# A new hand-written order, with weight groups loaded out of turn, in a gated linear attention followed by a gated MLP

## The chip, the core and the metric

The kernel runs on one core of a Trainium2 chip. The core has five engines with a queue of instructions each: TensorE (PE in the profile, with weight loads as PEld), VectorE (DVE), ScalarE (ACT), GpSimd (POOL) and SyncE (SP), which issues most transfers between device memory and on-chip memory. An engine takes its instructions in order. The metric is the device time of one execution in microseconds (us).

## The reference

```python
for t in range(S):                       # S = 768, for B = 4 batches and H = 8 heads, D = 48
    state = alpha[:, :, t, :, None] * state + einsum('bhd,bhe->bhde', k[:, :, t], v[:, :, t])
    y[:, :, t] = einsum('bhd,bhde->bhe', q[:, :, t], state)
x = y.transpose(0, 2, 1, 3).reshape(3072, 384)
g = x @ w_gate                           # 384 x 1536
h = g * (1 / (1 + exp(-g))) * (x @ w_val)
return (h @ w_out).astype(float32)       # 1536 x 384
```

Inputs of the attention are float32; the three weights are float64.

## The kernel before

**Attention.** The work is cut into 16 units of 192 tokens (a batch has four), each with all eight heads. A unit loads alpha, k and q (tasks `La`, `Lk`, `Lq`) and v (`V`, two buffers that alternate). Units 0 to 3 are transposed by TensorE (`Ta`, `Tk`, `Tq`, after a widening copy `pa`, `pk`, `pq`), the later ones by VectorE (`tr`, `tk`, `tq`). Two scans on VectorE (`G`, `f`) form running products of alpha; `mk` and `q` scale k and q by them. TensorE makes chunk scores (`S`), `ma` masks them, `B` or `Bw` carries the state on, and `Y` makes the outputs. Outputs are split into a high part and its residue (`yh`, `yl`) and packed into the layout of the MLP, for units 0 and 1 by TensorE (`R`, `x`), for the others by ten transfers (`xr`).

**MLP.** The 3072 tokens make 8 blocks of 384, and the 1536 hidden features 12 tiles f of 128: 96 steps. In a step PE makes the products `g` and `v` (nine matmuls each, since a product of two split numbers takes three); ACT makes `sl`, the silu of `g`; DVE makes `h`, its product with `v`; ACT rounds `h` to the high part `hh`, DVE or POOL makes the residue `hl`; PE adds the pair into the outputs (`o`, nine matmuls). Blocks 0 and 1 run in two halves (steps 0 to 6 are block 0 with f = 0 to 6, steps 7 to 13 block 1; steps 14 to 23 the rest), with half sums kept in device memory in between (`os`, `pl`); blocks 2 to 7 run through. Rows of outputs are copied from PSUM by `ot` and stored by `os`. In the profile a tile such as `h0_5` is block 0, f = 5.

**Weights.** The 36 weight tiles come in 20 groups: groups 0 to 2 hold one tile, the others two. Group p is loaded by `wl{p}` as pairs of 32-bit words and made a float32 by three passes over the words (`w{p}v0`, `v1`, `v2`; function `single`, L157 or L159, L165 or L169, L175); `w{p}a` rounds it to the high part (L343) and `w{p}p` forms the residue (L347). The raw words of group p lie where the finished group p + 1 will lie, so a group cannot be rounded before the next one's raw words have been used.

**Guards.** The fast path holds only for inputs in some range. All weights are loaded again and checked by ACT (`wr`, `wc`, 36 of each), and so is alpha, for each unit (`Lc`, `ck`: two passes, L456 and L457, summed into a column of `viol`). At the end DVE and PE reduce the sums to a flag (L921 to L932); every engine reads the flag (`values_load`, L1083) and branches on it (L1084) past a slow general path.

**What sets the order.** The string `ORDER` names all 1519 tasks in program order, as engine:task, with PSUM banks behind @ (t is TensorE, v VectorE, s ScalarE, g GpSimd, y SyncE). The program runs through it and issues each task on the engine named; each engine's queue is the part of the list that has its letter. Nothing else reorders the instructions.

Of the kernel before, what the change touches and what calls it, by code (L numbers as in the profile page):

```python
# [51 lines left out]
v:ma0.1 v:w1p s:ad0.2 t:Ta3@56 v:G2 y:Lk2 s:w4v0 t:Y0@01 y:Lq2 s:kc1.2 v:de1 s:kc1.1 y:wl10 v:f2 s:yh0.0 t:Bw1@3
s:yh0.1 y:V2 v:yl0.0 g:vc1 v:yl0.1 s:ad1.0 s:ad1.1 g:z2 v:ma1.0 t:R0.2@0 v:ma1.1 t:R0.1@1 v:w2p s:x0.2 t:Y1@47 s:ad1.2
v:w4v1 v:w4v2 s:w5v0 s:x0.1 v:w5v1 t:R0.0@0 v:w5v2 s:yh1.0 s:pk2 y:wl11 v:yl1.0 s:pq2 v:w3v2 t:Tk2@12 s:w5a t:Tq2@34
v:mk2 g:w4a s:w3a y:Lq3 y:wl12 s:x0.0 v:q2 g:w3p t:K2.2@1 s:yh1.1 t:K2.1@0 y:V3 s:kc2.2 t:K2.0@2 v:yl1.1 t:S2@34
s:kc2.1 v:de2 s:ea3 t:R1.1@0 v:ma2.2 g:pk3 t:R1.0@1 s:kc2.0 v:x1.1 t:R1.2@4 v:G3 s:x1.0 t:Tk3@02 s:x1.2 t:Bw2@1 s:pq3
y:wl13 s:vc2 v:mk3 y:wl14 s:w6v0 v:f3 t:Tq3@02 s:qc2 y:wl15 s:ad2.1 t:K3.1@4 t:g0 y:wl16 s:cq3 v:w6v1 y:wl17 s:kc3.1
t:v0 v:ma2.1 g:z3 g:q3 s:sl0 v:ma2.0 y:wl18 s:ad2.0 s:ad2.2 t:Y2@02 v:h0 s:qc3 v:de3 y:Lk4 s:hh0 v:w4p t:S3@13 s:yh2.0
s:yh2.1 v:w6v2 t:K3.0@4 t:K3.2@7 s:w7v0 t:g1 v:ma3.2 g:hl0 s:kc3.0 v:ma3.0 s:kc3.2 g:w6a v:yl2.0 t:v1 s:vc3 v:yl2.1
y:V4 g:w6p v:ma3.1 s:sl1 t:o0 v:h1 s:hh1 v:w5p t:Bw3@0 v:w7v1 s:w8v0 s:w9v0 v:w7v2 t:g2 v:w9v1 s:w7a s:ad3.0 s:ad3.1  # L60
v:w9v2 y:xr2 t:v2 v:w8v1 s:sl2 v:w8v2 t:Y3@01 v:h2 g:w7p s:w9a v:tk4 t:g3 s:hh2 s:yh3.0 s:yh3.1 g:hl1 v:yl3.0 s:w10v0
t:v3 v:yl3.1 v:w9p s:vc4 y:V5 t:o1 s:sl3 v:w10v1 s:w8a v:w10v2 t:g4 v:hl2 s:w10a v:h3 t:o2 v:w10p s:hh3 y:xr3 s:sl4
v:w8p t:v4 v:w11v0 v:w11v1 s:w12v0 t:g5 s:w13v0 v:h4 g:hl3 s:hh4 v:w13v1 t:v5 s:sl5 v:w13v2 t:g6 v:w11v2 y:La5 v:h5
g:hl4 s:w11a t:o3 v:w11p s:sl6 y:La4 t:o4 v:w12v1 s:hh5 s:w14v0 v:w12v2 t:v6 v:w14v1 s:w12a s:w13a v:w14v2 t:g7 v:h6
g:hl5 s:w14a t:v7 s:hh6 v:w14p s:sl7 g:hl6 t:g8 v:h7 g:w12p v:tr4 t:o5 s:sl8 y:Lq4 v:G4 s:w15v0 t:v8 s:hh7 t:o6 v:f4
t:g9 s:ot6.0 s:ot6.1 v:h8 g:hl7 y:os6.0 y:os6.1 s:hh8 t:v9 v:w15v1 s:sl9 v:hl8 t:g10 v:h9 g:z4 g:mk4 t:v10 s:ot6.2
s:sl10 v:w15v2 y:os6.2 t:o7 v:tq4 g:w15a g:w13p t:g11 v:kr4.2 s:hh9 y:Lk5 v:kr4.1 t:o8 g:hl9 s:w16v0 v:h10 g:q4 s:sl11
v:kr4.0 t:o9 s:hh10 v:kr4.3 g:qc4 t:v11 g:w15p v:tr5 t:g12 v:h11 y:Lq5 v:hl10 s:hh11 t:v12 v:G5 s:sl12 t:g13 v:f5
t:S4@01 t:B4@2 v:ma4.2 g:hl11 v:h12 t:o10 s:ad4.0 v:ma4.1 s:sl13 v:w16v1 t:o11 v:w16v2 s:hh12 v:ad4.1 g:hl12 s:w16a
t:v13 v:ad4.2 v:de5 t:o12 v:h13 v:w16p s:hh13 t:g14 v:hl13 v:w17v0 t:v14 v:z5 s:w18v0 y:wl19 v:w17v1 s:sl14 v:ma4.0  # L70
t:o13 v:h14 v:w18v1 s:hh14 t:Y4@01 v:w18v2 s:ot13.0 s:ot13.1 y:os13.0 v:w17v2 y:os13.1 t:g15 s:yh4.0 y:V6 v:tk5 g:w17a
s:vc5 g:hl14 t:v15 s:w18a v:yl4.0 s:sl15 v:w17p s:yh4.1 t:g16 s:ot13.2 v:w19v0 v:h15 g:mk5 y:os13.2 v:yl4.1 s:hh15
y:pl18.0 t:o14 s:sl16 y:La6 v:w19v1 t:v16 v:kr5.3 g:hl15 g:w18p v:tq5 t:o15 v:h16 y:Lk6 t:g17 g:q5 v:kr5.2 s:hh16
v:kr5.0 t:v17 s:sl17 g:qc5 v:hl16 t:g18 v:w19v2 v:h17 s:w19a v:tr6 s:hh17 t:v18 s:sl18 g:hl17 v:kr5.1 y:Lq6 t:o16
v:w19p v:h18 t:S5@01 y:xr4 v:tk6 s:hh18 t:B5@2 g:hl18 v:ma5.2 t:o17 v:ad5.0 v:ad5.1 t:o18 v:ad5.2 v:ma5.0 t:g19
v:ot18.0 v:ma5.1 y:pl18.1 v:G6 t:v19 y:La7 s:sl19 t:Y5@01 v:f6 y:os18.0 t:g20 s:yh5.0 y:V7 v:h19 g:vc6 s:yh5.1 v:yl5.0
# [106 lines left out]
def main_path(ctx, tc, q, k, v, alpha, w_gate, w_val, w_out, out, flag, spill):  # L183
# [137 lines left out]
    def weight_group(pieces):  # L321

        n = len(groups)
        groups.append(pieces)
# [1 line left out]
        is32 = w_gate.dtype == F32  # L330
# [785 lines left out]
```

## Time and profile before

| | before |
|---|---|
| times of three runs | 575.8, 572.19, 572.61 us, median 572.61 |
| the profiled execution: its span, from first to last instruction | 570.8 us |
| PE busy | 545.7 us, 96% of the span |
| DVE, ACT, POOL busy | 391.7, 280.5, 134.0 us |
| first `g` product | 51.67 us |
| end of the last matmul of the last `o` | 564.2 us |
| bytes moved | 77.66 MB, mean 136 GB/s |

The profile is of one execution. Its page gives the busy time of the engines, the busy tenths in 40 slices of the span (14.3 us each), the chain of work that ended last, and the costliest groups of instructions by line of the kernel. A group's row reads: line, engine, operation, out<-in, shapes, count | busy us, mean ns of one | idle before them, and what ended it. "L725" is line 725. The granted clock of TensorE was 0.99 on the mean of the span.

### The profile page before, as it was taken

To read this page: it belongs to the slowest core of one execution; us is meant where nothing else is said; L and a number is where in the kernel's file an instruction comes from. 1 tells how busy PE (TensorE), PEld (TensorE's weight loads), DVE (VectorE), ACT (ScalarE), POOL (GpSimd) and SP (SyncE) were. 2 spreads that over 40 slices of the span, in tenths; PEclk is the share of its full clock that TensorE was granted. 3 is DMA by queue.
4 is the path that set the end of the run, shared out by engine and by line. 5 is a ranking of instruction groups with operands and counts; after the bars stand their busy time and mean duration, and the time that the engine had idled before them with its cause. 6 is when DMAs were issued, how large, how long until landed. Compare 5 with 4: busy or idle time off the path is not lost.

```text
span 570.8 us, 13758 instructions
## 1 busy us (share of the span) xinstructions
PE 545.7 (96%) x5510; PEld 527.4 (92%) x5510; DVE 391.7 (69%) x601; ACT 280.5 (49%) x621; POOL 134.0 (23%) x152
## 2 busy tenths in 40 slices
PE   4779999999999999999999999999999999999995
...
DVE  6899998989989999889889698951793111210211
...
GB/s 204 309 318 254 277 82 112 115 40 108 131 146 146 135 132 107 124 126 113 93 100 187 172 156 205 191 141 89 218 111 85 116 132 86 97 73 121 41 2 47
DMA packets 95367, 77.66 MB, mean 136 GB/s; under 512 B 32832, under 2 KB 92224, under 8 KB 95296
## 3 DMA queue, kind: packets, MB, share of 16 engines
...
## 4 chain that ended last, share of the span: by engine, by line
PE 76%; DMA 10%; DVE 7%; SPq 3%; issue 2%; ACT 1%; DVEq 0%; ACTq 0%
PE ops L757 24%; PE v L725 23%; PE g L725 22%; DMA raw<-in_moe_w_out_dram 3%; DMA raw<-in_moe_w_gate_dram 2%; PE y L652 2%; PE A L580 2%; PE s L556 2%; DMA raw<-in_moe_w_val_dram 1%; DMA L<-in_k_dram 1%; DMA Le<-in_q_dram 1%; DVE K L531 1%; SPq L436 1%; PE y L635 1%; DVE t L165 1%
## 5 line engine op out<-in xcount | busy, mean ns | idle before, releaser
L725 PE MATMUL v<-xT,w 128*128 128x384 f32 x864 | 166.9, 337 | 3.2 <-DVE h L737 2.4
L725 PE MATMUL g<-xT,w 128*128 128x384 f32 x864 | 167.3, 337 | 0.4 <-ACT h L733 0.4
L757 PE MATMUL ops<-w,hh 128*128 128x384 f32 x576 | 159.8, 338 | 0.0
L725 PEld LDWEIGHTS v<-xT,w 128*128 128x128 f32 x864 | 150.7, 188 | 5.8 <-DVE h L737 3.4
L725 PEld LDWEIGHTS g<-xT,w 128*128 128x128 f32 x864 | 150.7, 188 | 1.4 <-ACT h L733 0.7
L737 DVE TENSOR_TENSOR h<-h,v 128x384 f32<-128x384 f32 x96 | 52.9, 551 | 120.1 <-PE v L725 92.5
L746 POOL TENSOR_TENSOR hl<-h,hh 128x384 fp32r<-128x384 f32 x57 | 65.5, 1150 | 264.7 <-ACT hh L741 263.5
L741 ACT CAST hh<-h 128x384 fp32r<-128x384 f32 x96 | 49.1, 511 | 128.1 <-DVE h L737 70.9
L757 PEld LDWEIGHTS ops<-w,hh 128*128 128x128 f32 x576 | 105.5, 188 | 1.0
L757 PE MATMUL ops<-w,hl 128*128 128x384 f32 x288 | 96.8, 336 | 0.0
L733 ACT ACTIVATE h<-g 128x384 f32<-128x384 f32 x96 | 46.9, 489 | 80.6 <-PE g L725 68.8
L531 DVE STREAM_TRANSPOSE K<-Gs 32x384 f32<-32x384 f32 x96 | 54.7, 570 | 2.3 <-PE A L580 0.4
L757 PEld LDWEIGHTS ops<-w,hl 128*128 128x128 f32 x288 | 54.1, 188 | 0.1
L746 DVE TENSOR_TENSOR hl<-h,hh 128x384 fp32r<-128x384 f32 x39 | 22.9, 589 | 14.8 <-ACT hh L741 14.6
L590 DVE TENSOR_TENSOR X<-s,mask 64x384 f32<-64x384 f32 (+1 forms) x48 | 26.3, 552 | 8.5 <-PE s L556 7.6
L471 DVE TENSOR_TENSOR_SCAN AT<-AT,back 128x771 f32<-128x771 f32 x16 | 30.9, 1933 | 0.6
L462 DVE TENSOR_TENSOR_SCAN Gs<-AT,inj 128x772 f32<-128x772 f32 x16 | 28.7, 1794 | 0.1
L417 PE MATMUL pt<-ident,wide 128*128 128x128 f32 x72 | 14.9, 376 | 11.4 <-POOL mask L243 5.1
L417 PEld LDWEIGHTS pt<-ident,wide 128*128 128x128 f32 x72 | 12.1, 197 | 13.4 <-ACT wide L405 5.1
L319 ACT ACTIVATE wc<-wc,wbias 128x384 f32<-128x384 f32 x36 | 23.4, 650 | 1.2
L318 ACT ACTIVATE wc<-wc,wbias 128x384 f32<-128x384 f32 x36 | 23.3, 648 | 1.2
L839 POOL TENSOR_TENSOR Gs<-trk,Gs 128x768 f32<-128x768 f32 x10 | 17.9, 1785 | 25.3 <-DVE Gs L462 13.8
(118 smaller groups left out, 608.4 us busy)
## 6 DMA issues: line engine op xcount, KB each, us to landing
...
```

Source lines behind the costliest of these rows:

```text
L319: nc.scalar.activation(dev, dev, AF.Relu, bias=wbias[:, 1:2], accum_out=wviol[:, 0, i : i + 1])
L417: nc.tensor.transpose(pt[:, j - js.start, :], Wd.rearrange("p j e c -> p (j e c)")[:, j * P : (j + 1) * P], ident)
L462: nc.vector.tensor_tensor_scan(*(x.rearrange("p g t -> p (g t)")[:, ::-1] for x in (Gs, AT, inj)), 0.0, op0=ALU.mult, op1=ALU.add)
L471: nc.vector.tensor_tensor_scan(Af, Af, back[:, 1 : n + 1], back[:, 0:1], op0=ALU.mult, op1=ALU.add)
L531: nc.vector.transpose(out=bass.AP(k0.tensor, k0.offset, [k0.ap[0], (G * 2 * D, NU), (2 * D, G), (1, 32)]), in_=Kg[j * BO + x : j * BO + x ...
L590: nc.vector.tensor_tensor(out=X[r, z, f * GF : (f + 1) * GF, :].rearrange("r g (c t) -> r g c t", c=NU), in0=sps[f][r].rearrange("r g (c t ...
L725: nc.tensor.matmul(pt, wsp[kind, f][a][:, kt * P : (kt + 1) * P], xT[blk][:, b_, kt, :], start=(n == 0), stop=(n == 3 * KT - 1),)
L733: nc.scalar.activation(h, acc.pop(("g", blk, f)), AF.Silu)
L737: nc.vector.tensor_tensor(out=h, in0=h, in1=acc.pop(("v", blk, f)), op=ALU.mult)
L741: nc.scalar.copy(out=hh, in_=acc["h", blk, f])
L746: eng.tensor_tensor(out=hl, in0=acc.pop(("h", blk, f)), in1=hh.bitcast(F32), op=ALU.subtract)
L757: nc.tensor.matmul(ops[blk][i], h[b_][:, i * P : (i + 1) * P], wsp["o", f][a], start=(first and n == 0), stop=(last and n == 2),)
```

## The change

`ORDER` is replaced by another list of the same 1519 tasks. `weight_group` is handed its group's number, where it counted its calls before, so that the loads can stand in any order: it is now 0, 1, 3, 2, 6, 4, 9, 5, 14, 10, 7, 13, 8, 11, 12, 16, 15, 18, 17, 19. The lines behind move up by three (L347 is L344 now, L737 is L734).

By the list, tasks change engines: the residues of groups 0, 1, 2, 4, 10, 11, 14, 16 and 17 go from DVE to POOL, those of 7 and 12 from POOL to DVE; the first cuts of groups 1, 11, 17 and 19 go from DVE to ACT, that of group 0 from ACT to DVE; POOL makes 63 residues `hl` instead of 57; DVE makes 15 copies `ot` instead of 6 and 9 `mk` instead of 6. The load of v for unit 2 stands behind six weight loads on SP's queue, where it stood behind ten. The weight checks `wc` are spread over earlier steps, and the alpha check `ck15` stands at the end of the list.

```diff
@@ -44,97 +44,96 @@
 ORDER = """
-y:La0 y:wl0 y:Lk1 y:La1 y:Lq0 y:V1 s:pa0 t:Ta0@01 s:w0v0 v:w0v1 s:ea0 v:w0v2 y:Lk0 s:w0a v:G0 s:pa1 y:Lq1 s:pq0 y:La2
...
-v:h89 s:hh89 t:v90 s:sl90 v:hl89 t:o89 v:h90 s:hh90 v:hl90 t:g91 t:v91 s:ck14 t:o90 s:sl91 s:ck15 v:h91 t:g92 s:hh91
...
-s:os95.2
+y:La0 s:pa0 y:wl0 t:Ta0@73 y:La1 s:ea0 y:Lq0 s:pa1 y:Lk0 v:w0v0 v:w0v1 v:w0v2 v:G0 t:Ta1@50 s:pq0 s:w0a y:Lq1 y:Lk1
...
+t:o94 y:os83.1 t:o95 v:ot95.0 s:ck13 s:ot95.2 y:os95.0 v:ot95.1 y:os95.1 s:os95.2 v:z15 s:ck15
 """
@@ -282,7 +281,7 @@
     HSEG = 7
-    wsp, groups, wtiles = {}, [], []
+    wsp = {}
     wlist = [("g", 0), ("v", 0)]
     for f in range(1, NF):
@@ -318,14 +317,12 @@
         nc.scalar.activation(dev, dev, AF.Abs, bias=wbias[:, 0:1])
         nc.scalar.activation(dev, dev, AF.Relu, bias=wbias[:, 1:2], accum_out=wviol[:, 0, i : i + 1])
-    def weight_group(pieces):
-        n = len(groups)
-        groups.append(pieces)
+    def weight_group(n, pieces):
         size = len(pieces) * NB
         is32 = w_gate.dtype == F32
         each = NB if is32 else 2 * NB
@@ -871,7 +868,7 @@
     def named_weights(p):
         def load(eng):
-            wfns[p] = weight_group(wgroups[p])
+            wfns[p] = weight_group(p, wgroups[p])
         todo[f"wl{p}"] = load
         if w_gate.dtype != F32:
```

DVE's queue around the sixth and seventh hidden tile of block 0 (`h0_5`, `h0_6`; t11 is the cut of group 11, w11 its split form). Before:

```order
L175 SCALAR_TENSOR_TENSOR t11_1263<-raw11_641,t11_1263 128x768
L737 TENSOR_TENSOR h0_5_1296<-h0_5_1296,v0_5_1286 128x384
L347 TENSOR_TENSOR w11_1317<-t11_1263,w11_1317 128x768
L165 SCALAR_TENSOR_TENSOR t12_1266<-raw12_672,t12_1266 128x768
L175 SCALAR_TENSOR_TENSOR t12_1266<-raw12_672,t12_1266 128x768
L165 SCALAR_TENSOR_TENSOR t14_1348<-raw14_819,t14_1348 128x768
L175 SCALAR_TENSOR_TENSOR t14_1348<-raw14_819,t14_1348 128x768
L737 TENSOR_TENSOR h0_6_1329<-h0_6_1329,v0_6_1351 128x384
```

The same place now:

```order
L174 SCALAR_TENSOR_TENSOR t11_1235<-raw11_947,t11_1235 128x768
L734 TENSOR_TENSOR h0_5_1267<-h0_5_1267,v0_5_1247 128x384
L164 SCALAR_TENSOR_TENSOR t12_1260<-raw12_1034,t12_1260 128x768
L174 SCALAR_TENSOR_TENSOR t12_1260<-raw12_1034,t12_1260 128x768
L394 STREAM_TRANSPOSE trk4_1298<-L1_72 128x4x6x32
L734 TENSOR_TENSOR h0_6_1322<-h0_6_1322,v0_6_1284 128x384
```

The residue of group 11 has left this queue and the cut of group 14 stands behind `h0_6`; the transpose of unit 4's k has come forward.

POOL's queue ahead of the first `hl` (w2 to w4 are weight groups, `wide` a widened unit, X1 the scaled q, L0 and L1 buffers of loads). Before:

```order
L343 CAST w4_667<-t4_458 128x768
L347 TENSOR_TENSOR w3_669<-t3_390,w3_669 128x768
L405 COPY wide_79<-L1_72 128x12x48
L475 MEMSET AT_86 128x3
L490 TENSOR_TENSOR X1_104<-trq3_858,AT_86 112x768
L388 MEMSET L1_72 128x4x32
L746 TENSOR_TENSOR hl0_0_992<-h0_0_880,hh0_0_937 128x384
```

The same place now:

```order
L340 CAST w3_650<-t3_301 128x768
L344 TENSOR_TENSOR w3_650<-t3_301,w3_650 128x768
L402 COPY wide_79<-L1_72 128x12x48
L344 TENSOR_TENSOR w2_613<-t2_529,w2_613 128x384
L487 TENSOR_TENSOR X1_104<-trq3_739,AT_86 112x768
L344 TENSOR_TENSOR w4_840<-t4_601,w4_840 128x768
L385 MEMSET L0_71 128x4x32
L385 MEMSET L1_72 128x4x32
L743 TENSOR_TENSOR hl0_0_984<-h0_0_838,hh0_0_956 128x384
```

The residues of groups 2 and 4 are new here (those of groups 0 and 1 are further up), the rounding of group 4 has gone to ACT, and two memsets of unit 4's loads stand behind group 4's residue.

ACT's queue at the end of the main path (`ops` are the PSUM banks of the outputs, ac13 and ac15 the alpha checks of units 13 and 15). Before:

```order
L741 CAST hh7_10_6784<-h7_10_6737 128x384
L741 CAST hh7_11_6807<-h7_11_6772 128x384
L769 COPY ot7_0_11_6820<-ops7_0_0_6462 128x384
L769 COPY ot7_1_11_6822<-ops7_1_0_6463 128x384
L769 COPY ot7_2_11_6825<-ops7_2_0_6464 128x384
L774 DMA out_0_dram<-ot7_2_11_6825 128x384
L1083 TENSOR_LOAD flag_60
L1084 COMPARE_AND_BRANCH
```

The same place now:

```order
L738 CAST hh7_11_6790<-h7_11_6753 128x384
L453 ACTIVATE ac13_6786<-ac13_6786,nbias_112 128x576
L454 ACTIVATE ac13_6786,viol_110<-ac13_6786,dbias_114 128x576
L766 COPY ot7_2_11_6819<-ops7_2_0_6445 128x384
L771 DMA out_0_dram<-ot7_2_11_6819 128x384
L453 ACTIVATE ac15_6751<-ac15_6751,nbias_112 128x576
L454 ACTIVATE ac15_6751,viol_110<-ac15_6751,dbias_114 128x576
L1080 TENSOR_LOAD flag_60
L1081 COMPARE_AND_BRANCH
```

Two of the three copies of the last outputs have gone to DVE; the check ac13 stands ahead of the third, and the check ac15 between the last store and the reading of the flag.

More of the change, by code (lines that the diff above doesn't have):

```diff
@@ L52 @@
[L52 to L76, printed above, removed]
@@ new lines @@
+v:w3v2 s:kc1.2 v:z2 y:wl6 s:pa3 t:Bw1@4 s:yh0.0 s:w2v0 g:w1p t:Ta3@56 y:wl4 s:vc1 v:yl0.0 s:ad1.1 s:yh0.1 g:pk2
+t:Y1@23 g:pq2 v:w2v1 y:V2 s:ad1.2 v:w2v2 s:w4v0 s:yh1.0 t:Tk2@41 s:w2a s:yh1.1 v:yl0.1 t:R0.1@0 v:mk2 t:Tq2@74 v:q2
+t:R0.0@1 t:K2.0@7 v:yl1.0 y:Lk3 t:R0.2@4 s:x0.0 s:ea3 v:yl1.1 g:w3a s:kc2.0 y:Lq3 s:x0.2 s:pq3 v:x0.1 y:wl9 t:K2.2@2
+t:R1.2@5 t:R1.0@6 t:R1.1@0 v:de2 t:K2.1@4 s:x1.1 v:w4v1 s:x1.0 g:w3p y:wl5 g:pk3 y:wl14 y:V3 t:Tk3@13 y:wl10 s:x1.2
+g:w2p t:Tq3@70 v:G3 v:ad0.0 t:g0 s:kc2.1 v:w4v2 v:f3 s:kc2.2 s:cq3 s:w6v0 t:v0 s:w5v0 s:vc2 t:S2@70 v:w5v1 y:wl7 s:qc2
@@ new lines @@
+t:o2 s:hh3 v:w10v2 s:yh3.1 g:hl3 t:g5 v:yl3.1 v:h4 s:w11v0 t:o3 v:w9p t:v5 s:w10a g:w10p s:w12v0 v:tr4 s:hh4 v:w11v1
+v:w11v2 s:sl5 v:h5 t:g6 v:w12v1 v:w12v2 s:w14v0 t:v6 g:hl4 s:hh5 v:tk4 t:o4 s:w11a g:w11p y:xr3 s:sl6 t:g7 v:h6 v:G4
+s:hh6 s:kc3.2 s:w12a s:w13v0 t:v7 g:hl5 y:Lq4 s:sl7 v:mk4 y:wl16 t:o5 v:w12p v:h7 t:g8 v:f4 g:hl6 g:z4 s:sl8 t:v8 t:g9
+v:w14v1 s:hh7 v:hl7 y:wl15 v:w14v2 v:h8 s:sl9 t:o6 v:ot6.2 v:tq4 s:ot6.0 y:wl18 t:v9 s:hh8 t:g10 v:h9 v:w13v1 g:hl8
+s:w15v0 t:v10 v:w15v1 y:os6.0 v:q4 g:qc4 s:sl10 v:w15v2 s:ot6.1 t:g11 v:w13v2 y:La5 s:w13a t:o7 s:hh9 v:h10 y:os6.1
@@ new lines @@
+s:yh6.0 s:sl26 s:yh6.1 y:pl23.2 v:tr8 s:qc7 v:ot23.1 v:kr7.1 t:g27 v:h26 t:v27 g:hl25 v:yl6.1 s:sl27 v:ot23.2 t:g28
+t:o24 s:hh26 t:o25 v:kr7.3 v:h27 v:tk8 v:yl6.0 v:hl26 s:hh27 g:hl27 v:G8 t:v28 y:os23.1 s:sl28 v:kr7.0 y:V7 t:g29
+s:sl29 t:S7@02 v:f8 v:de7 v:ma7.0 t:B7@1 y:xr6 v:h28 y:wr0 t:o26 s:hh28 v:ma7.1 t:o27 t:v29 v:ad7.0 v:h29 t:g30
+v:ad7.1 v:ma7.2 g:hl28 s:sl30 t:v30 y:V8 v:mk8 s:hh29 s:vc7 t:Y7@02 t:g31 v:kr8.3 v:kr8.0 t:o28 v:hl29 v:h30 s:sl31
+s:hh30 y:wr10 v:kr8.1 y:Lq8 t:v31 v:kr8.2 v:h31 s:yh7.0 y:La9 v:tq8 t:o29 v:yl7.0 v:hl30 y:V9 y:Lk9 s:yh7.1 g:z8 t:g32
@@ new lines @@
+v:tq10 s:ot35.0 s:wc10 v:kr10.2 t:v38 s:sl38 v:h38 v:ma9.2 t:g39 v:ad9.0 y:os35.1 s:hh37 v:ad9.1 y:La11 v:ma9.0
+s:ot35.2 g:hl37 y:Lk11 s:sl39 t:v39 s:wc0 t:o36 v:f10 s:hh38 t:o37 s:vc9 v:h39 v:kr10.0 g:z10 g:q10 t:g40 y:wr2 s:qc10
+g:hl38 v:tr11 v:ma9.1 t:v40 s:sl40 s:hh39 t:g41 y:V10 g:hl39 v:ad9.2 t:S10@12 y:Lq11 v:h40 v:tk11 v:ma10.2 v:ma10.1
+t:o38 t:v41 v:kr10.1 v:G11 s:sl41 v:ad3.0 t:Y9@02 y:wr4 v:mk11 v:h41 s:hh40 s:yh9.0 t:o39 s:wc2 v:de10 v:hl40 t:g42
+t:o40 s:hh41 s:sl42 v:hl41 t:v42 v:kr10.3 v:yl9.0 s:wc4 v:h42 t:B10@0 s:yh9.1 v:yl9.1 t:g43 t:v43 v:ad10.0 v:ma10.0
@@ new lines @@
+g:hl47 v:ma11.1 t:g49 t:o47 v:h48 y:xr10 s:sl49 v:kr12.1 t:v49 v:ma11.2 s:hh48 v:ma11.0 y:wr8 t:Y11@21 s:ot47.1
+s:ot47.0 t:g50 s:yh11.0 y:os47.1 v:h49 v:kr12.2 t:v50 g:z12 s:hh49 v:hl48 s:yh11.1 v:yl11.0 v:hl49 v:kr12.3 y:Lk13
+s:sl50 v:ot47.2 t:g51 t:o48 v:q12 v:tr13 v:h50 s:sl51 s:wc7 t:g52 s:hh50 y:wr5 v:yl11.1 y:xr11 t:o49 t:v51 g:vc12
+y:Lq13 v:tk13 t:S12@01 v:hl50 s:wc5 v:G13 t:B12@2 y:V13 v:ma12.2 v:mk13 s:sl52 t:o50 s:ad12.0 v:h51 v:ad12.1 v:kr13.2
+t:g53 v:ma12.1 g:qc12 s:hh51 g:hl51 t:v52 s:sl53 v:ad12.2 t:o51 v:h52 v:ma12.0 t:g54 s:hh52 t:v53 t:Y12@12 v:hl52
@@ new lines @@
+v:tq13 v:h53 s:wc8 t:v54 v:kr13.1 s:hh53 g:hl53 v:kr13.0 s:sl54 y:wr12 y:La14 v:h54 t:o52 v:de13 v:f13 t:g55 v:z13
+t:v55 s:hh54 s:sl55 v:h55 t:o53 t:v56 g:hl54 g:q13 v:kr13.3 s:yh12.0 s:yh12.1 t:g56 v:yl12.0 v:tr14 y:wr16 s:wc16
+y:wr20 s:hh55 t:o54 t:S13@01 v:yl12.1 s:sl56 v:h56 t:B13@2 v:G14 s:hh56 t:g57 v:ad13.0 s:wc12 g:hl56 s:sl57 y:Lk14
+t:v57 v:hl55 t:o55 v:ad13.1 v:f14 v:h57 y:os47.2 y:Lq14 v:ma13.2 v:ad13.2 t:g58 y:os47.0 y:wr11 t:v58 g:qc13 s:wc11
+g:vc13 v:ma13.1 v:ma13.0 s:sl58 y:wr22 t:Y13@01 s:hh57 g:hl57 v:h58 s:wc20 t:v59 y:wr17 s:yh13.0 v:yl13.0 s:yh13.1
```

121 lines of the change are left out of this document (58 added, 63 removed).

## The prediction

> **What bounds the kernel now.** I read the page first: its span, and the busy tenths of two engines.
>
> ```profile
> span 570.8 us, 13758 instructions
> ...
> PE   4779999999999999999999999999999999999995
> ...
> DVE  6899998989989999889889698951793111210211
> ```
>
> TensorE (PE) is full from the third slice on, so the time is PE's own work plus what PE waits. Next the busy time in three stretches: until the first product of the MoE part (`g0`, at 51.6 us), from there to the start of `g7`, and from there to the last matmul. The columns are the stretch, its length, then PE, PEld, DVE, ACT and POOL busy.
>
> ```profile
> 0.00:51.60 51.60, 36.75 (x699) 32.20 (x700) 42.68 (x65) 38.09 (x82) 12.60 (x36) 0.93 0.93 272
> 51.60:91.60 40.00, 38.11 (x426) 35.70 (x424) 37.01 (x44) 25.55 (x51) 14.06 (x14) 1.00 0.66 181
> 91.60:564.30 472.70, 470.87 (x4390) 459.50 (x4388) 312.04 (x494) 216.44 (x490) 107.30 (x102) 1.00 0.45 118
> ```
>
> PE idles 14.85 us in the first stretch, 1.89 in the second, 1.83 in the third: after 91.6 us nothing but these 1.8 us can be won. What holds PE before that is told by the chain of waits, from 82 us on (start, length, what):
>
> ```profile
> 82.61 0.55 DVE h L737
> 83.16 0.88 DVE t L165
> ...
> 85.64 0.95 DVE t L175
> ...
> 86.62 0.84 ACT w L343
> ...
> 92.78 0.56 DVE h L737
> ...
> 93.38 1.86 PE v L725 x9
> ```
>
> The chain runs along VectorE (DVE): weight cuts (L165, L175), the residue of a split weight (L347), and `h`, on which the next `v` product waits. In the first two stretches DVE is busy 42.7 + 37.0 = 79.7 of 91.6 us. So the front of the program is as long as what stands ahead of `h` in DVE's queue. Behind it PE runs full, and what is won in the front is won at the end, less what the tail costs.
>
> **The front.** The rows of the order in the section on the change show DVE's queue between `h0_5` and `h0_6` (the sixth and seventh hidden tiles of block 0): the residue of group 11 is gone from it, and the cut of group 14 stands behind. POOL's rows ahead of the first `hl` show where residues went: those of groups 0, 1, 2 and 4 are new there. I count DVE's queue up to `h8`, since up to `v9`, which waits for it, PE has the same tasks in both. The durations are means of the first 100 us (group, count, busy, mean ns):
>
> ```profile
> L175 DVE SCALAR_TENSOR_TENSOR t<-raw,t 128x768 uint32<-128x768 uint32 x12 | 13.5, 1131 | 0.3
> L165 DVE SCALAR_TENSOR_TENSOR t<-raw,t 128x768 uint32<-128x768 uint32 x11 | 12.4, 1124 | 0.5 <-ACT t L157 0.4
> ...
> L746 POOL TENSOR_TENSOR hl<-h,hh 128x384 fp32r<-128x384 f32 x7 | 9.6, 1372 | 22.1 <-ACT hh L741 20.9 <-DMA raw<-in_moe_w_out_dram 1.2
> ...
> L347 DVE TENSOR_TENSOR w<-t,w 128x768 fp32r<-128x768 f32 x7 | 8.3, 1196 | 0.9 <-ACT w L343 0.9
> ...
> L347 POOL TENSOR_TENSOR w<-t,w 128x768 fp32r<-128x768 f32 x4 | 8.1, 2031 | 4.7 <-ACT w L343 4.6
> ...
> L490 POOL TENSOR_TENSOR X<-trq,AT 112x768 f32<-112x768 f32 x1 | 1.7, 1697 | 0.9 <-ACT trq L810 0.9
> ...
> L347 DVE TENSOR_TENSOR w<-t,w 128x384 fp32r<-128x384 f32 x3 | 1.6, 544 | 0.0
> ...
> L839 DVE TENSOR_TENSOR Gs<-trk,Gs 128x768 f32<-128x768 f32 x1 | 1.0, 959 | 0.1
> L490 DVE TENSOR_TENSOR X<-trq,AT 112x768 f32<-112x768 f32 x1 | 1.0, 958 | 0.1
> ...
> L746 DVE TENSOR_TENSOR hl<-h,hh 128x384 fp32r<-128x384 f32 x1 | 0.6, 554 | 0.0
> L159 DVE TENSOR_SCALAR t<-raw 128x768 uint32<-128x768 uint32 x1 | 0.6, 552 | 0.0
> ```
>
> Out of the queue ahead of `h8` go the residues of groups 0 to 2 (3 x 0.54 = 1.6) and of 4, 10, 11 and 14 (4 x 1.20 = 4.8), `q1` (1.0), and the two steps of the cut of group 13 (1.12 + 1.13 = 2.25): 9.65. The first step of group 11's cut goes to ACT too (0.55, L159); together 10.2. Into it come the residues of groups 7 and 12 (2.4), `mk4` (1.0, L839), and one `hl` more (0.55): 3.95. Net DVE has 6.2 us less to do.
>
> At `h8` DVE before had a little to spare:
>
> ```profile
> 95.35 0.56 DVE L737 TENSOR_TENSOR h<-h,v 128x384 f32<-128x384 f32 x1 [0.63 <-PE v L725]
> 96.71 1.68 DVE L397 STREAM_TRANSPOSE AT<-L 128x768 f32<-128x768 f32 x1 [0.80 <-DMA L<-in_alpha_dram]
> ```
>
> It waited 0.63 + 0.80 = 1.4 us between `h6` and `h8`, so against the place that did bind, `h6`, the gain is 6.2 + 1.4 = 7.6 us. PE can take that: it idled 16.7 us up to `g7`.
>
> Against it stands that DVE's operations are slower beside POOL's:
>
> ```profile
> 66.94 2.61 POOL L347 TENSOR_TENSOR w<-t,w 128x768 fp32r<-128x768 f32 x1 [4.60 <-ACT w L343]
> ...
> 67.78 2.59 DVE L165 SCALAR_TENSOR_TENSOR t<-raw,t 128x768 uint32<-128x768 uint32 x1
> ```
>
> That cut takes 0.88 to 0.95 us in the chain's rows; here, beside a residue on POOL, 2.59. The three groups of DVE with two inputs (L175, L165, L347) lie above 0.96 (what `q1` and `mk4` took for the same width) by 12 x 0.17 + 11 x 0.16 + 7 x 0.24 = 5.5 us, while POOL worked 9.6 + 8.1 + 1.7 = 19.4 us with two inputs: 0.28 us lost on DVE for each us of POOL. By `h8` POOL has more: residues of groups 0 to 2 (3 x 1.0, half of the wide one) and 4, 10, 11, 14 (4 x 2.03), `q1` 1.7, less groups 7 and 12 (4.06) and an `hl` (1.4): 7.4 us. At 0.28 DVE loses 2.1; at the worst row, 1.64 lost in the 1.77 us in which both ran (0.93), 6.9; at best nothing. I take the mean of the stretch, 2.1.
>
> So the front gives -7.6 + 2.1 = -5.5 us, with ends of -7.6 and -0.7.
>
> The Trainium skill (GPSIMD Engine Reference, section 1, Specifications) speaks against such a move: GpSimd shares its SBUF interfaces with VectorE and contends with Vector instructions that have two SBUF inputs. The row of 2.59 agrees, the mean of 0.28 only in part. If each us of such work were taken from DVE again, as that rule alone would have it, the front would give about -0.7 and the sum would be +2.1.
>
> Two moves are hidden, I think. The load of unit 2's V, which waits for unit 0's outputs, stood behind ten weight groups on SP's queue and stands behind six now, so groups 9, 5, 14, 10, 7 and 13 start up to 15 us later. Their cover is DVE, which cuts them one by one until 92 us; without it each us late costs one. ACT gets three more first cuts and loses copies that move to DVE in the last third, where DVE has room.
>
> **The middle.** One wait in the long third stretch is DVE's again (total, times, longest):
>
> ```profile
> PE v L725 <- DVE h L737: 1.7, 2, 1.2
> ```
>
> With over 6 us less in DVE's queue the longer goes: -1.2. A new order can add stalls of this size; the bounds are -1.8 (all idle gone) and +2.
>
> **The tail.** The guard on alpha for one unit, `ck15`, is two ACT passes; its sum goes into a flag on which every engine branches at the end. As the rows of ACT's end show, `ck15` (tile ac15) moves from `h` of step 91 to behind the last store, and the flag behind it; `ck13` still fits beside the last products. What each takes, from ACT, DVE, the flag's lines and the chain's end:
>
> ```profile
> 540.82 0.77 ACT L456 ACTIVATE ac<-ac,nbias 128x576 f32<-128x576 f32 x1
> ...
> 542.31 0.19 ACT L457 ACTIVATION_READ_ACCUMULATOR ac<-ac,dbias 128x1 f32 x1
> ...
> 564.79 0.38 ACTq L774 DMA_DIRECT2D out_dram<-ot  x1
> ```
> ```profile
> 542.53 0.16 DVE L921 TENSOR_REDUCE vsa<-viol 128x1 f32<-128x16 f32 x1
> ...
> 543.12 0.16 DVE L927 TENSOR_TENSOR oka<-oka,oks 128x1 f32<-128x1 f32 x1
> ```
> ```profile
> L1083 SPq TENSOR_LOAD <-flag x1: 480/480/480, 547.4 to 547.4; - x1
> ...
> L1083 SPq SEQ_ASSERT  x1: 37/37/37, 548.5 to 548.5; - x1
> ```
> ```profile
> L1084 SPq EVENT_SEMAPHORE  x8: 17/17/17, 568.9 to 569.4; - x8
> ...
> L1084 SPq COMPARE_BRANCH  x1: 50/50/50, 565.4 to 565.4; - x1
> ```
> ```profile
> 559.50 4.70 PE ops L757 x27
> ```
>
> The last matmul ends at T = 564.2. ACT's store is issued by 565.2, T + 1.0. Then `ck15`, 540.82 to 542.50 = 1.7; DVE's four small operations, 542.53 to 543.28 = 0.8; a one-column matmul and a cast, about 0.5 (an estimate, three times the 0.16 of the small ones); SP's reading of the flag until its branch, 547.4 to 548.6 = 1.2. SP branches at T + 5.2. Before, it had read the flag at 547 and branched at 565.4, T + 1.2, and the next thing it did came 3.5 us later. So the end comes 4.0 us later against PE's. Below, if only ACT's part counts, 3.0; above, 4.7.
>
> **The sum.** -5.5 - 1.2 + 4.0 = -2.7 us on the span of 570.8: 568.1. The median of the times, 572.6, is 1.8 above that span, which I take as what lies around it: 569.9.
>
> **The rivals.** All of DVE's relief arrives, the middle is clean and the tail costs its lower end: -7.6 - 1.8 + 3.0 = -6.4, 566.2. For it: DVE's operations at their bare 0.95 us; against: POOL is busier just there.
>
> The port takes it back: at 0.93 the front gains 0.7, the middle keeps its wait, the tail costs 4.0: +3.3, slower, 575.9; with a stall of 2 us, 577.9. The place is DVE's queue from 40 to 90 us, and it decides from about 0.5 us lost for each us of POOL (7.6 - 7.4 x 0.5 = 3.9, the tail's price). For it: the row of 2.59; against: the mean of 0.28.
>
> The front is not DVE's to give: DVE waits for loads or for ACT as much as it is relieved, and only the tail changes: +4.0, 576.6. For it, the busy time by stretch (its last columns are the clock, the DMA engines' share and GB/s):
>
> ```profile
> 20.00:40.00 20.00, 15.07 (x434) 13.58 (x428) 18.36 (x27) 15.68 (x39) 1.99 (x5) 0.91 1.08 360
> ```
>
> The loads are at their full share just there. Against: DVE is busy 18.4 of these 20 us, and the chain behind is DVE's.
>
> **How the numbers follow.** Forecast 0.48; all relief 0.22; port 0.15; tail alone 0.12; the rest 0.03. The forecast's own range is 566.8 to 573.5. The range reaches from 565 to 578: it leaves out the lowest of the second case and the worst of the third. Faster by over 1% (under 566.9, about what a measurement can tell from no change) is the second case and a little of the first: 0.24. Slower by over 1% (over 578.3) is part of the third and fourth: 0.11. The rest is 0.65.
>
> **What would show it.** Right: `g0` starts before 47 us and `g7` before 87; the last matmul ends near 557.5; between it and SP's branch stand `ck15`, the reduction and the flag, and the span ends 10 to 11 us behind PE instead of 6.6. Wrong: `v` products of steps 1 to 12 wait for `h` as before, with cuts of over 1.2 us on DVE; or the chain goes through transfers of raw weights in 45 to 90 us; or PE idles more than 2 us behind `g7`.

## The result and the profile after

The change takes 566.55 us (median of ten runs, 563.2 to 572.2; the two longest, 571.9 and 572.2, ran in the chip's slower state and are not in the ratio) against 573.38 us before (ten runs, 571.4 to 575.8). The ratio is 0.9883 with a 95% interval of 0.9857 to 0.9909: 1.2% faster, 6.8 us, where 2.7 us were forecast. The profiled execution of the change is one of its longest (571.53 us, granted clock 0.984), so its trace shows the loss of an unlucky run; the front of a usual one is better seen in `tail_early`, an experiment below whose order is the same up to the last steps.

The page of the change, its span, the busy tenths of TensorE (PE) and VectorE (DVE) in 40 slices, and the chain of waits by engine:

```profile
span 569.8 us, 13778 instructions
...
PE   4798999999899999999999999999999999999993
...
DVE  7978699989997878888897887845584312121222
...
PE 90%; DVE 4%; issue 3%; ACT 1%; DMA 1%; ACTq 0%; DVEq 0%
```

The same row of the page before has another make-up:

```profile
PE 76%; DMA 10%; DVE 7%; SPq 3%; issue 2%; ACT 1%; DVEq 0%; ACTq 0%
```

DVE's share of the chain fell by 3 points, that of transfers (DMA) by 9 and that of SP's issuing by 3. That is a first sign, and a weak one, that it was not DVE that was relieved.

To cut the span into front, middle and tail I take the start of `v8` (the `v` product of step 8), up to which both programs have the same 1155 matmuls, and the end of the last matmul. Busy time in the three stretches (the stretch, its length, then PE, PEld, DVE, ACT, POOL, the granted clock, the DMA engines' share and GB/s), before:

```profile
0.00:98.25 98.25, 81.05 (x1155) 73.78 (x1156) 84.44 (x113) 67.57 (x138) 29.84 (x52) 0.97 0.80 225
98.25:564.20 465.95, 464.68 (x4356) 453.62 (x4355) 307.28 (x489) 212.50 (x482) 104.12 (x100) 1.00 0.45 118
564.20:570.80 6.60, 0.00 (x0) 0.00 (x0) 0.00 (x0) 0.48 (x1) 0.00 (x0) 0.65 0.29 98
```

and after:

```profile
0.00:94.20 94.20, 79.17 (x1155) 73.70 (x1156) 79.02 (x107) 63.07 (x132) 42.79 (x55) 0.95 0.80 220
94.20:559.69 465.49, 462.81 (x4354) 453.09 (x4353) 306.02 (x487) 212.01 (x480) 112.04 (x104) 1.00 0.47 121
559.69:569.80 10.11, 0.19 (x2) 0.11 (x2) 0.87 (x7) 2.12 (x4) 0.00 (x0) 0.63 0.20 66
```

The front is 4.05 us shorter, the middle 0.46, and the tail 3.5 longer: 1.0 us on the span of these two executions. In the front PE idles 15.0 us instead of 17.2. The front of `tail_early` (564.96 us):

```profile
0.00:89.59 89.59, 77.09 (x1155) 70.71 (x1156) 80.76 (x107) 63.39 (x132) 43.72 (x55) 0.98 0.81 218
```

It is 8.7 us shorter than before: PE is busy 4.0 us less and idle 4.7 us less. Two stalls of the change's profiled execution stand out in PE's rows (start, length, what, and in brackets the idle time before it):

```profile
29.71 1.37 PE L577 MATMUL A<-V,K 128*48 128x48 f32 x30 [3.00 <-issue]
...
58.06 0.49 PE L553 MATMUL s<-X,Gs 48*64 48x64 f32 x6 [2.90 <-issue]
```

Both fall into the middle of one task, between small matmuls that wait for no other engine. In each a block of 16 KB of code, taken to be PE's, is on its way (from 27.24 to 28.18 and from 55.44 to 56.75 us), and PE goes on 1.3 to 1.5 us after it has landed. Three stalls in other profiles end 1.35 to 1.41 us behind such a block too (before at 38.0 us, `tail_early` at 26.5, `residues_left_out` at 59.8). The clock is granted at half for 3.4 us from 29.8 and for 6.8 us from 57.1. So two blocks of code that came late seem to have cost this execution nearly 6 us of stall and some more of half clock.

### The profile page after: what moved, and what is told of

Same layout as the page of the kernel before. It is cut to its first block, busy times and chain, and to the rows that moved or that the text cites. A ratio compares the mean times of both kernels' runs of the same rounds, so it can differ in the third digit from the quotient of the medians.

```text
span 569.8 us, 13778 instructions
## 1 busy us (share of the span) xinstructions
PE 542.2 (95%) x5510; PEld 526.9 (92%) x5510; DVE 385.9 (68%) x599; ACT 277.2 (49%) x616; POOL 154.8 (27%) x159
## 4 chain that ended last, share of the span: by engine, by line
PE 90%; DVE 4%; issue 3%; ACT 1%; DMA 1%; ACTq 0%; DVEq 0%
PE g L722 26%; PE ops L754 26%; PE v L722 26%; PE A L577 3%; PE y L649 2%; PE s L553 2%; PE y L632 1%; PE y L633 1%; DVE Gs L459 1%; PE kps L512 1%; PE pt L414 1%; PE s L577 1%; DMA Le<-in_alpha_dram 1%; PE xp L689 0%; DVE AT L468 0%
## 5 line engine op out<-in xcount | busy, mean ns | idle before, releaser
L743 POOL TENSOR_TENSOR hl<-h,hh 128x384 fp32r<-128x384 f32 x63 | 72.4, 1151 | 298.8 <-ACT hh L738 298.7
L734 DVE TENSOR_TENSOR h<-h,v 128x384 f32<-128x384 f32 x96 | 53.1, 554 | 112.5 <-PE v L722 96.9
L743 DVE TENSOR_TENSOR hl<-h,hh 128x384 fp32r<-128x384 f32 x33 | 19.8, 601 | 20.9 <-ACT hh L738 20.8
L487 POOL TENSOR_TENSOR X<-trq,AT 112x768 f32<-112x768 f32 x10 | 18.1, 1808 | 33.4 <-DVE AT L468 11.4
L344 POOL TENSOR_TENSOR w<-t,w 128x768 fp32r<-128x768 f32 (+1 forms) x14 | 25.9, 1852 | 4.4 <-ACT w L340 4.0
L577 PE MATMUL A<-V,K 64*48 64x48 f32 (+1 forms) x720 | 23.3, 217 | 3.9 <-issue 3.0
L577 PEld LDWEIGHTS A<-V,K 64*48 64x48 f32 (+1 forms) x720 | 20.7, 132 | 5.0 <-issue 3.6
L317 ACT ACTIVATE wc<-wc,wbias 128x384 f32<-128x384 f32 x36 | 23.5, 651 | 1.2
```

What stands on the lines that cost most here:

```text
L344: eng.tensor_tensor(out=lo, in0=src, in1=hi.bitcast(F32), op=ALU.subtract)
L577: nc.tensor.matmul(to[j * BO : j * BO + D, g - gs.start, :], Ks[r, x, g, KC[j]], Vd[r, x, g, VC[j]], start=(x == 0 or not whole), stop=(x ...
L734: nc.vector.tensor_tensor(out=h, in0=h, in1=acc.pop(("v", blk, f)), op=ALU.mult)
L743: eng.tensor_tensor(out=hl, in0=acc.pop(("h", blk, f)), in1=hh.bitcast(F32), op=ALU.subtract)
```

## The experiments

All twelve, with the time (median), the ratio to the kernel before run beside it, and from each profile: the start of `v8`, PE's busy and idle time up to it, the DMA engines' share from 20 to 40 us (it adds up the time of the packets, so it can pass 1), and the tail (last matmul of the last `o` to the end of the span). The kernel before took 572.9 to 574.0 us beside them.

| kernel | us | ratio, 95% | `v8` | PE busy | PE idle | DMA share | tail |
|---|---|---|---|---|---|---|---|
| before | 573.4 | 1 | 98.3 | 81.1 | 17.2 | 1.08 | 6.6 |
| residues_pool | 573.5 | 0.999 to 1.003 | 100.2 | 80.7 | 19.4 | 1.08 | 6.2 |
| residues_left_out | 572.8 | 0.997 to 1.001 | 99.6 | 80.5 | 19.1 | 1.07 | 6.2 |
| v1_late | 573.4 | 0.999 to 1.002 | 97.4 | 79.3 | 18.1 | 1.09 | 5.2 |
| warm_before | 574.3 | 1.001 to 1.004 | 99.4 | 76.2 (without the idle matmuls) | 23.2 | 1.07 | 8.1 |
| guard_late | 579.1 | 1.008 to 1.012 | 98.7 | 80.6 | 18.1 | 1.05 | 11.5 |
| change | 566.6 | 0.986 to 0.991 | 94.2 | 79.2 | 15.0 | 0.71 | 10.1 |
| tail_early | 565.0 | 0.984 to 0.988 | 89.6 | 77.1 | 12.5 | 0.71 | 8.2 |
| residues_dve | 567.9 | 0.989 to 0.995 | 87.7 | 75.6 | 12.1 | 0.90 | 10.6 |
| v1_early | 567.8 | 0.988 to 0.993 | 90.9 | 79.0 | 11.9 | 0.71 | 10.8 |
| loads_in_turn | 567.8 | 0.987 to 0.993 | 88.3 | 77.1 | 11.1 | 0.73 | 10.2 |
| scores_first | 568.6 | 0.990 to 0.995 | 89.4 | 76.6 | 12.8 | 0.89 | 11.2 |
| guards_early | 584.6 | 1.016 to 1.024 | 88.1 | 76.9 | 11.2 | 0.85 | 6.6 |
| warm_tail | 562.7 | 0.979 to 0.985 | 87.8 | 73.1 (without the idle matmuls) | 14.7 | 0.83 | 7.6 |

The upper six have before's order, the lower eight that of the change. No edit to the one kind moves `v8` to where the other kind has it: 97 to 100 us there, 88 to 94 here.

### The tail

`tail_early` and `guard_late` move one task, `ck15`, in the change and in the kernel before.

```diff
 the change's order, at its end (tail_early)
-s:sl95 t:o92 t:v95 v:h95 t:o93 s:hh94
+s:sl95 t:o92 t:v95 v:h95 t:o93 s:ck15 s:hh94
...
-s:os95.2 v:z15 s:ck15
+s:os95.2 v:z15
 the order before, at its end (guard_late)
-t:o90 s:sl91 s:ck15 v:h91
+t:o90 s:sl91 v:h91
...
-s:os95.2
+s:os95.2 s:ck15
```

> The changed kernel with one task moved: the alpha check of unit 15 (ck15) stands ahead of hh94 on ScalarE instead of behind the last store. In the profile of the changed kernel the span ended 10.1 us behind the last matmul (559.7 to 569.8), before the change 6.6 us. If the check, the reduction and the flag on the path are what the tail costs, the end comes 3.5 us closer to the last matmul (about 6.6) and the time falls from 566.6 to about 563. Rival: the end is set by fetching the code behind the branch, whenever the flag is read; then the time stays at 566 to 567.

> The kernel before with one task moved: ck15 behind the last store on ScalarE, as in the change. If the tail costs what the two profiles show, 3.5 us (the prediction said 4.0, with 3.0 to 4.7): 576.4 to 578. Rival, as for the other tail run: no change, 573.4.

`guard_late` came to 579.1, a ratio of 1.010: 5.7 us, more than the 3.5 expected and above the expected 576.4 to 578; its tail is 11.5 us in the profile, 4.9 longer, and in that execution the middle is 2.5 us longer as well. `tail_early` gave 565.0, 1.6 us less than the change, between what was expected (563) and the rival (566 to 567), and its interval overlaps that of the change; its tail is 8.2, 2.0 us shorter than the change's and not 3.5, since `ck13` still ends late and the reduction and the one-column matmul stand behind the last products. What is on the path is shown by the end of the chain of waits of the change (start, length, what):

```profile
559.72 0.49 ACT ot L766
...
560.23 0.38 ACTq L771
...
560.65 0.79 ACT ac L453
...
561.46 0.88 ACT ac L454 x2
...
562.36 0.18 DVE vsa L918
...
563.25 0.20 PE cps L928 x2
...
563.48 0.15 DVE flag L929
```

Every engine then branches, and PE's branch alone took 3.9 us:

```profile
L1081 PEldq COMPARE_BRANCH  x1: 3902/3902/3902, 564.3 to 564.3; - x1
```

From SP's branch to the end of the span it took 4.8 to 6.9 us in the different profiles. Blocks of code are fetched there (one of 16 KB from 565.3 to 566.9 us in the change); why it varies isn't settled.

`guards_early` was to give the whole tail back: all 104 loads and checks of the guards behind the same products as before.

```diff
 one of 104 moves: each wr, wc, Lc and ck stands where its product has it in the order before
-s:os95.2 v:z15 s:ck15
+s:os95.2 v:z15
...
-t:o90
+t:o90 s:ck15
```

> The changed kernel with all loads and checks of the guards (wr, wc, Lc, ck) behind the same products of TensorE as in the kernel before, so that the flag is read long before the last store. The span should then end 6.6 us behind the last matmul as before, not 10.1, and 8.2 as with ck15 alone moved: 562.5 to 563.5, 3 to 4 us faster than the change. Rival: the checks now delay the silus or the copies in the middle, and what is won in the tail is lost there: 565 or more.

Its tail is 6.6 us, as before the change, and so the late flag is what the tail costs. But the time is 584.6, since PE idles 15.5 us in the middle, where the change idles 2.7, and its busy time there is 471.6 us instead of 462.8:

```profile
88.07:575.15 487.08, 471.61 (x4356) 458.14 (x4355) 306.61 (x492) 213.10 (x483) 113.59 (x104) 0.99 0.45 118
```

The rival named in the expectation was right, and its size was not foreseen. Checks that stand right behind a product on ScalarE (ACT) wait there for their own loads and hold up the silu, for which PE waits:

```profile
492.44 0.77 ACT L452 ACTIVATE ac<-ac,nbias 128x576 f32<-128x576 f32 x1 [2.93 <-DMA ac<-in_alpha_dram]
```
```profile
494.95 2.55 PE L721 MATMUL g<-xT,w 128*128 128x384 f32 x7 [2.41 <-ACT h L729]
```

Silus are a part of it: by engine and producer, PE's two largest waits in this stretch are for packed attention outputs on their way (`xT`) and for silus.

```profile
PE g L721 <- DMA xT<-X: 4.4, 3, 1.9
...
PE g L721 <- ACT h L729: 3.5, 3, 2.4
```

What made the outputs late is not shown. The order before has the checks behind the same products without such waits; there they stand behind other work of ACT. The change's spread of the checks is worth keeping; only its last few are badly placed.

### Residues on GpSimd

The prediction rested on this. Three runs: the residues of seven groups back on DVE in the change, on GpSimd (POOL) in the kernel before, and left out of it (the products then read the high part in the residue's place).

```diff
 the change's order (residues_dve)
-g:w0p g:w1p g:w2p g:w4p g:w10p g:w11p g:w14p
+v:w0p v:w1p v:w2p v:w4p v:w10p v:w11p v:w14p
 the order before (residues_pool)
-v:w0p v:w1p v:w2p v:w4p v:w10p v:w11p v:w14p g:w7p g:w12p
+g:w0p g:w1p g:w2p g:w4p g:w10p g:w11p g:w14p v:w7p v:w12p
 the kernel before (residues_left_out)
-                wsp[piece] = tuple(parts[0][:, x, i * NB : (i + 1) * NB] for x in range(2))
+                wsp[piece] = tuple(parts[0][:, 0 if n in LEFT else x, i * NB : (i + 1) * NB] for x in range(2))
...
-v:w0p v:w1p v:w2p v:w4p v:w10p v:w11p v:w14p
```

> The changed kernel with the residues of groups 0, 1, 2, 4, 10, 11 and 14 on VectorE again, at the same places of the list. The prediction's theory (VectorE's queue sets the front, and its relief is the gain): 3 x 0.54 + 4 x 1.2 = 6.4 us come back on VectorE, less up to 2 us of contention that goes: plus 4 to 6 us, 571 to 573, with v products of the first steps waiting for h again. Rival (the front is set by the order of TensorE's own work and of the loads, and VectorE has room): within 1.5 us of 566.6.

> The kernel before with only the engines of the residues as in the change: groups 0, 1, 2, 4, 10, 11 and 14 to GpSimd, 7 and 12 to VectorE, all at their old places. The prediction's theory: VectorE has 6.4 - 2.4 = 4.0 us less in the front, less some contention: 2 to 4 us faster than before (573.4), 569.5 to 571.5. Rival (order, not relief): within 1 us of 573.4, or slower because GpSimd's slower residues then stand ahead of what waits for them.

> The kernel before without the residues of groups 0, 1, 2, 4, 10, 11 and 14; the products of these groups read the high part where they read the residue, so that TensorE does the same work (the low bits of these weights are left out). VectorE has 6.4 us less to do and GpSimd nothing more. The prediction's reading of the chain (VectorE's queue sets the front): v8 starts about 6 us earlier than 98.3, and the time falls to about 567 to 568. Rival (the front is set by TensorE's idle time and half-clock time, which this hardly touches): v8 within 2 us of 98.3, and the time within 2 us of 573.

`residues_dve` took 567.9, 1.3 us more than the change, with overlapping intervals; its `v8` even starts earlier than in the other profiles. `residues_pool` took 573.5: nothing. Its DVE has five instructions less up to `v8` and works as long as before, 84.4 us, while POOL works 8.3 us more:

```profile
0.00:100.15 100.15, 80.73 (x1155) 73.64 (x1156) 84.40 (x108) 67.22 (x138) 38.15 (x57) 0.98 0.78 221
```

The groups show where the relief went. The six steps of the decay of the carried state, on DVE too, took 434 ns each before and 872 ns here (count, busy us, mean ns):

```profile
L619 DVE SCALAR_TENSOR_TENSOR V<-SE,Gs 48x192 f32<-48x192 f32 x6 | 2.6, 434 | 0.1
```
```profile
L617 DVE SCALAR_TENSOR_TENSOR V<-SE,Gs 48x192 f32<-48x192 f32 x6 | 5.2, 872 | 0.1
```

So POOL took back all of the 4.0 us. In the order of the change it is the same: with seven residues back on DVE (`residues_dve`) DVE works 81.5 us up to `v8`, in `tail_early` 80.8. `residues_left_out` has no such price: DVE works 77.8 us up to `v8` instead of 84.4, and PE's waits for `h` in the products `v` fall from 2.4 to 1.1 us. Its time is 572.8, `v8` at 99.6:

```profile
0.00:99.64 99.64, 80.50 (x1155) 73.46 (x1156) 77.76 (x106) 67.26 (x138) 30.13 (x52) 0.98 0.79 222
```

What came in its place is one stall, of the kind seen above:

```profile
PE v L725 <- issue: 2.5, 1, 2.5
PE v L725 <- DVE h L737: 1.1, 1, 1.1
```

The stall is of this one execution; that the time stays is of twelve runs. Over 6 us less in DVE's queue do not shorten the front.

### The start and the loads

New theory: the first units' inputs come earlier. On SP's queue the six transfers of V1 stood ahead of the k of unit 0. `v1_late` and `v1_early` move V1 alone, `loads_in_turn` puts the weight loads of the change into ascending order at the same places.

```diff
 the order before (v1_late)
-y:Lq0 y:V1 s:pa0
+y:Lq0 s:pa0
...
-y:V0
+y:V0 y:V1
 the change's order (v1_early)
-y:Lq0 s:pa1
+y:Lq0 y:V1 s:pa1
...
-s:ad0.1 y:V1
+s:ad0.1
 the change's order (loads_in_turn)
-wl0 wl1 wl3 wl2 wl6 wl4 wl9 wl5 wl14 wl10 wl7 wl13 wl8 wl11 wl12 wl16 wl15 wl18 wl17 wl19
+wl0 wl1 wl2 wl3 wl4 wl5 wl6 wl7 wl8 wl9 wl10 wl11 wl12 wl13 wl14 wl15 wl16 wl17 wl18 wl19
```

> The kernel before with one task moved: the load of unit 1's v (V1, six transfers that took 4.24 to 8.16 us on SP's queue) stands behind unit 0's v instead of ahead of unit 0's k. New theory (the front is set by how early the first units' inputs come): k of unit 0 is issued at 4.2 instead of 8.2 us, the second scan starts about 2.9 us earlier as in the change (16.19 to 13.29), and the time falls by 2 to 4 us, 569 to 571. Rival (VectorE's queue is full from 20 us on and keeps its length): within 1 us of 573.

> The changed kernel with only V1 moved back to where it stood, ahead of unit 0's k on SP's queue. New theory: the start is 3 to 4 us later again, 568.5 to 571. Rival (the start doesn't matter, what follows has slack): within 1 us of 566.6.

> The changed kernel with the 20 weight loads at the same places of SP's queue but in ascending order, as before the change. If the order of the loads is part of the gain (groups come as the cuts take them), cuts wait for raw words and the time rises by 2 us or more, over 568.5. If the start and the order of the compute queues make the gain, it stays within 1.5 us of 566.6.

573.4, 567.8 and 567.8: nothing on the kernel before, and 1.3 us on the change each time, less than the 2 us that were to tell it, with intervals that overlap. The theory of the start falls for the kernel before, and in the change neither the start nor the order of the loads, the only thing that the change needed new code for, has an effect that is clear of the noise.

### The clock and TensorE's order

Rows of the same 48 score matmuls of unit 0 show another difference. Before, and in the change:

```profile
18.84 1.47 PE L556 MATMUL s<-X,Gs 48*64 48x64 f32 x48
```
```profile
15.19 0.93 PE L553 MATMUL s<-X,Gs 48*64 48x64 f32 x48
```

Before, the records of the granted clock begin with full speed at 20.1 us, in the change at 12.8; until then the array seems to run at half, as the longer row shows, although the view by stretch, which knows nothing earlier, shows 1.00. Up to `v8` the time at half clock, with all that lies ahead of the first record, is 20.1 + 6.8 = 26.9 us before, 23.0 in the profiled change, 15.3 in `tail_early` and 12.0 in `residues_dve`, and PE is busy 81.1, 79.2, 77.1 and 75.6 us for the same matmuls: (81.1 - 75.6) / (26.9 - 12.0) = 0.37 us for each us at half clock. `warm_before` and `warm_tail` put 19 matmuls of zeros into PE's idle time at the start.

```diff
+    def fill(x, n):
+        pt = ps.tile([P, P], F32, tag="A2", name=f"fill{x}")
+        for _ in range(n):
+            nc.tensor.matmul(pt, inj[:, 0, 0:P], inj[:, 1, 0:P], start=True, stop=True)
...
-t:Ta0
+t:fill0 t:Ta0 t:fill1
```

> The kernel before with 19 idle matmuls more (128x128 of zeros, into a bank that is free then), 12 ahead of the first transpose and 7 behind it, in TensorE's idle time at the start. In the profile of before the clock is granted in full from 20.1 us, in that of the change from 12.8 us; 48 score matmuls took 1.47 us there and 0.93 here. Theory (half clock is part of the difference): full clock from about 8 to 10 us, TensorE's work up to v8 some 3 us shorter (81.1 to 78), and the time 1 to 3 us less, 570 to 572. Rival (TensorE only waits the longer for the rest): within 0.5 us of 573, or slower.

> The changed kernel with ck15 moved (as in tail_early, 565.0) and the same idle matmuls at the start. Full clock from about 8 us instead of 11.9: TensorE's work in 8 to 12 us is some 1 us shorter, so 563.5 to 565. Rival: no change against 565.0, or slower because the idle matmuls delay the first transposes.

The first twelve took 4.8 to 5.3 us and put the first transpose off by 1.3 to 1.9 us. Even so `warm_tail` took 562.7, 2.2 us less than `tail_early` and the fastest of all (the two intervals overlap by 0.001): full clock from 5.7 us, no half-clock time behind it up to the tail, and PE's own work up to `v8` 4.0 us shorter, of which 1.8 us arrive at `v8`. `warm_before` had a like gain of work (76.2 us instead of 81.1) and no gain of time (574.3): PE idles 23.2 us instead of 17.2, and 1.9 of these 6.0 us can be the late first transpose. So in the change PE's work sets a part of the front. Before the change shorter work only makes PE wait longer, and what it waits for is not the residues on DVE either.

The last run undoes a part of PE's order: S2 and Bw2 of unit 2 ahead of the first products again.

```diff
 the change's order
-t:g0 s:kc2.1 v:w4v2 v:f3 s:kc2.2 s:cq3 s:w6v0 t:v0 s:w5v0 s:vc2 t:S2@70 v:w5v1 y:wl7 s:qc2 t:Bw2@2
+s:kc2.1 s:kc2.2 s:cq3 s:vc2 t:S2@70 t:Bw2@2 t:g0 v:w4v2 v:f3 s:w6v0 t:v0 s:w5v0 v:w5v1 y:wl7 s:qc2
```

> The changed kernel with one part of TensorE's order undone: the scores and the carry of unit 2 (S2, Bw2), with the four ScalarE copies that they need, stand ahead of the first products g0 and v0 again, as before the change. In the profile of the change g0 starts at 42.06 us, while the last of those copies ends at 44.3. Theory (the front became shorter because products now stand where attention steps wait for copies, so TensorE idles less): TensorE idles about 2.3 us ahead of S2, and the time rises by 2 to 3 us, to 568.5 to 569.6. Rival (TensorE has slack in the front): within 1 us of 566.6.

568.6, 2.0 us more. PE waits for the copy, as the theory has it, a little less long than it said:

```profile
40.58 1.48 PE L552 MATMUL s<-X,Gs 48*64 48x64 f32 x48 [1.60 <-ACT trq L806]
```

and the clock is at half for 3.4 us behind it (the 48 matmuls take 1.48 us). The intervals of this run and of the change overlap by 0.001 (0.990 and 0.991), so the 2 us are likely, not certain. The profile doesn't show them in the front: `v8` starts at 89.4, within the 87.7 to 90.9 of the other runs of this order.

### What stays open

The front is 4 us shorter in the profiled change and 7 to 11 in the other profiles of its order. Of that the order of S2 and Bw2 may explain some 2. The rest may lie in when the weights are loaded. In the kernel before, the chain of waits runs through transfers of raw weights in its first 62 us, of which these four (start, length) are the longest up to 51 us:

```profile
15.29 5.60 DMA raw<-in_moe_w_gate_dram
...
20.91 7.96 DMA raw<-in_moe_w_gate_dram
...
28.89 8.43 DMA raw<-in_moe_w_out_dram
...
44.21 6.76 DMA raw<-in_moe_w_out_dram
```

From 20 to 40 us its DMA engines move 360 GB/s, and in the change, which has only six groups ahead of unit 2's V where before had eleven (0 to 10; the section on the change and the prediction say ten), 190:

```profile
20.00:40.00 20.00, 16.45 (x412) 14.57 (x408) 15.84 (x27) 14.63 (x38) 8.96 (x9) 0.91 0.71 190
```

All six kernels with before's order have a share of 1.05 to 1.09 there, all eight with the new one 0.71 to 0.90. That goes with the theory, but everything else of the two orders differs too. Nor does the chain of waits settle it: transfers have 6 to 10% of it in five of the six, but 1% in `residues_pool`, which is no faster. The run that would tell, the order before with five groups' loads moved behind V2, was not made. So what made the front shorter is in the main open.

## Why the prediction was right or wrong

**Its number.** 569.9 was forecast and 566.55 measured, inside the range of 565 to 578; faster by over 1% had a chance of 0.24. That the number came near is in part luck. The tail was right for the reason given, but the front was to shrink by relief of DVE, and it shrank by something else and by more: 8.7 us in `tail_early`. With that front, the middle (-0.46) and the tail (+3.5) the sum is -5.6 us, near the measured 6.8.

**The bound.** The reading of the chain was the first mistake. It was read from 82 us on, where it runs along DVE; up to 70 us it runs in the main through loads, and the page gave 10% of it to DMA against 7% to DVE. A chain through DVE also doesn't say how long PE waited there: for `h`, 2.4 us in all products `v` together.

**The front (-5.5).** The step that failed is "PE can take that: it idled 16.7 us up to `g7`". Of these, 14.85 us lay ahead of `g0`, where the residues of the large groups don't stand. With 6.4 us less on DVE and nothing more on POOL nothing changed (`residues_left_out`). The 1.4 us that were added to the relief are waits too, 0.63 for PE and 0.80 for a load of alpha, and a load doesn't land earlier because DVE has less to do. The front did become shorter, by 4.05 us in the two profiles: PE idled less (17.2 to 15.0 us, in `tail_early` 12.5) and ran at half clock for a shorter time (26.9 to 23.0 us, in `tail_early` 15.3). The clock was no term of the sum. Why PE idled less is the open question above.

**POOL and DVE (+2.1).** The price of 0.28 us for each us of POOL was too low: in `residues_pool` POOL's 8.3 us more took back the whole 4.0 us of relief, 0.48. That is the point from which the port rival was to decide. Its mechanism was there, but as the front wasn't DVE's, nothing was lost by it in the time. The rule of the Trainium skill that was weighed there (GPSIMD Engine Reference, section 1, Specifications) agrees with the doubled 872 ns.

**The middle (-1.2).** It became 0.46 us shorter. A wait for `h` of 1.1 us is there still, and a new one of 1.6 us has come, as the waits of the whole execution show:

```profile
PE s L553 <- DVE X L667: 1.6, 1, 1.6
...
PE v L722 <- DVE h L734: 1.1, 1, 1.1
```

PE idles 2.7 us there instead of 1.3. That its busy time is lower by 1.9 us, so that the middle did not become longer for it, is not explained.

**The tail (+4.0, 3.0 to 4.7).** Right: 3.5 us in the two profiles, by the steps that were named. Moved alone, the check cost 5.7 us, above the upper bound; 4.9 us are in the tail of that profile.

**The signs.** `g0` starts at 42.06, before 47, as forecast for the right case; `g7` at 87.94, not before 87; the last matmul ends at 559.7 in the profiled execution (forecast 557.5) and 555.1 in `tail_early`; the span ends 10.1 us behind it (10 to 11). PE's waits for `h` are not as before, 1.1 us instead of 2.4, and yet they were not what counted. One sign of being wrong did come: PE idles more than 2 us behind `g7` (2.7).

**Half clock.** The Trainium skill (TensorE: Matmul & The Clock Gate, Part 1) says that half speed is the idle state and that about 3.4 us of activity release it, in a window that runs freely. The traces agree: every spell at half clock between two matmuls lasted 3.4 or 6.8 us, and the kernel that kept PE busy at the start had full clock from 5.7 us.
